# In the second round, the adding transfers of the first weights' lower parts are ordered behind the token gather on GpSimd

## The chip, the cores and the metric

The kernel runs on one core of a Trainium2 chip. The metric is the device time of one execution in microseconds (us). Five engines with a queue of instructions each work in order: TensorE (PE in the profile, its weight loads PEld), VectorE (DVE), ScalarE (ACT), GpSimd (POOL) and SyncE (SP). SyncE starts plain transfers; GpSimd starts indexed ones (gather, scatter) and those that add to what the destination holds. An engine waits for another, or for a transfer, by semaphores.

## What is computed

The reference is an attention followed by a mixture of experts:

```python
scores = scale * np.matmul(q, k.transpose(0, 1, 3, 2))
...
attn = np.exp(scores)
attn = attn / (np.sum(attn, axis=-1, keepdims=True) + 1e-09)
...
order = np.argsort(-flat)
for idx in order:
    tok, e = (int(idx) // E, int(idx) % E)
    if assigned[tok] >= 0 or counts[e] >= cap:
        continue
    assigned[tok] = e
    counts[e] += 1
...
for e in range(E):
    mask = assigned == e
    h = np.maximum(x[mask] @ w1[e], 0.0)
    out[mask] = h @ w2[e]
```

There are 4608 tokens of 512 numbers, 8 experts with 1024 hidden units, and each expert takes exactly 576 tokens. Attention masks are a window of 32 positions, or a dilated one (every fourth of 128).

## The kernel before

The attention fills the first 205 us or so and leaves its result xd in HBM. Then come eight rounds, numbered r = 0 to 7 in the code; the second round is r = 1. Each finds the next expert that fills up (`search`: counts on TensorE from flags G that VectorE makes, eight times in a row, each waiting for the other), lists its 576 tokens (`settle`, `listing`: the index list idx), fetches them (`gather`, line 1258: five indexed transfers xg, four of 128 rows and one of 64), transposes them on TensorE (line 1272, into the one buffer ptx), splits them into a high part xh (ScalarE) and the rest xl (VectorE), and runs two matrix products: the first with w1 into ph (line 1309), the second with w2 into py (lines 1351 to 1356). Results y go out by an indexed store each (line 1377). The search for round r + 1 runs while round r computes, so while TensorE still does the second product of r = 0, the tokens and first weights of r = 1 come in.

Every weight tile is split as well: raw is loaded by SyncE (line 1159), ScalarE makes the high part h (w1h, w2h), and the lower part l (w1l, w2l) is raw - h. For the three sets in `ADDED`, w2 of r = 0 and w1 and w2 of r = 1, ScalarE writes -h into l (line 1167) and GpSimd starts a transfer that adds raw to it (line 1169); the others are subtracted on VectorE. In the round r = 1 the loads of w1 from the fifth tile on (`AHEAD_W`), and all of SyncE's loads behind them, stand behind a gate: a one-element MEMSET on GpSimd (line 1150) that waits for the second gather to be issued.

The order of instructions on an engine is not written by hand. `op(engine, cost, fn, deps, boost)` notes an operation; `Schedule.run` goes through a modelled time and takes, for each engine, the ready operation with the earliest due time. A due time is the modelled end less `left`, the longest chain of costs and latencies that still follows the operation, less its boost. So an operation that gains a follower becomes due earlier. `deps` also becomes a wait where the program needs one; for an order between two instructions of one engine none is needed.

Of the buffers that the loads fill, eight raw buffers serve w1, four serve w2; a raw buffer is free again when the adding transfer has read it (`use.append(lo)`).

Of the kernel before, what the change touches and what calls it, by code (L numbers as in the profile page):

```python
# [14 lines left out]
OP = mybir.AluOpType  # L15
# [16 lines left out]
NM = 5  # L32
# [6 lines left out]
B_L, B_G, B_T, B_X, B_H, B_HL, B_Y, B_S, B_W = 23000, 27000, 15000, 0, 20000, 17000, 28000, -15000, 1500  # L39
RAW1, D_R, NQ, AHEAD_W = 8, 262, (2, 2), (3, 4)  # L40
ADDED, T_A, T_G = (("2", 0), ("1", 1), ("2", 1)), 4500, 4500
# [114 lines left out]
class Schedule:  # L156
# [8 lines left out]
    def op(self, eng, cost, fn, deps=(), boost=0, lat=0, dma=0, buf=None):  # L165
        x = Op(len(self.ops), eng, cost, fn, deps, boost, lat, dma, buf)
        for d in x.deps:
            d.users.append(x)
        self.ops.append(x)
        return x  # L170
# [940 lines left out]
def moe(tc, ctx, C, R, xd, w1, w2, out):  # L1111
    nc = tc.nc
# [7 lines left out]
    op = K.op  # L1120
# [22 lines left out]
    E, gemm1_end, x_users, got, gate = {}, {}, {}, {}, {}  # L1143

    def weights(n, r, f, deps):

        raw, old, use = RAW[n].take()
        if n == "1" and r < len(AHEAD_W) and f == AHEAD_W[r]:

            gate[r] = op("POOL", 100, lambda: nc.gpsimd.memset(raw[:1, :1], 0.0), [got[r, 1], *old], B_G)  # L1150
        if r in gate:
            deps = [*deps, gate[r]]

        def load():
            if n == "1":
                src = w1[bass.ds(E[r], 1), f].rearrange("o p d f -> p (o d f)")
            else:
                src = w2[bass.ds(E[r], 1), f * 128:f * 128 + 128, :].rearrange("o p d -> p (o d)")
            nc.sync.dma_start(raw, src)

        ld = op("SP", 60, load, [*deps, *old], dma=T_W)
        h, oldh, useh = WH[n].take()
        l, oldl, usel = WL[n].take()
        hi = op("ACT", 525, lambda: act(h, raw), [ld, *oldh], B_W)
        if (n, r) in ADDED:
            use.append(hi)
            ne = op("ACT", 525, lambda: nc.scalar.activation(l, h.bitcast(F32), AF.Copy, scale=-1.0), [hi, *oldl], B_W)
            useh.append(ne)
            lo = op("POOL", 1040, lambda: nc.gpsimd.dma_start(l, raw, accum_op=OP.add), [ne], B_W, lat=T_A)
            use.append(lo)  # L1170
        else:
            lo = op("DVE", 600, lambda: sub(nc.vector, l, raw, h), [ld, hi, *oldl], B_W)
            use += [hi, lo]
        useh.append(lo)
        return h, l, hi, lo, useh, usel
# [216 lines left out]
    def round_(r):  # L1392
        e = None
        if r:
            e = search(r) if r < NE - 1 else chain("DVE", 650, R.last, [st["fetch"], st["need"]])
        en = st["fetch"] = EN[r] = op("SP", 100, lambda: fetch(r, R.eidx), [e])
        ix, BOX[r] = settle(r, e)
        X[r] = gather(r, ix, BOX[r])
        W[r] = [weights("1", r, f, [en]) for f in range(NF)]

    round_(0)
    for r in range(NE):
        W2 = [weights("2", r, f, [EN[r]]) for f in range(NF)]
        expert(r, X[r], BOX[r], W[r], W2)
        if r + 1 < NE:
            round_(r + 1)
# [78 lines left out]
```

## Time and profile before

| | us |
|---|---|
| median of 3 runs (lowest, highest) | 705.41 (704.57, 706.64) |
| the profiled execution, its own time | 708.44 |
| its span, from the first to the last instruction | 706.6 |
| mean granted clock of TensorE | 0.972 |
| TensorE busy | 665.0 |
| VectorE busy | 484.7 |
| ScalarE busy | 291.4 |
| GpSimd busy | 140.6 |

The span is what the profile's views cover; its own time holds 1.84 us around it. Times in the rows are us from the start of the span. A granted clock of 1.00 is 2.4 GHz, 0.50 is 1.2 GHz. In the timeline a row is one instruction, or several of one kind (x9), and brackets give the idle time of the engine before it and who ended that.

### The profile page before, as it was taken

How to read it: one execution, taken by the hardware profiler on the slowest of the kernel's cores; microseconds unless marked ns; L12 is line 12 of the kernel's file. 1: busy time of each engine (PE TensorE's matmuls, PEld its weight loads, DVE VectorE, ACT ScalarE, POOL GpSimd, SP SyncE). 2: the span in 40 equal slices, each digit the busy share in tenths (PEclk: the TensorE clock that was granted, in tenths of full speed). 3: DMA queues.
4: the chain of work that ended last, by engine and by line, in shares of the span. 5: the costliest groups of instructions: out<-in, count | busy, mean ns of one | idle time of the engine just before them, and what ended most of it. 6: DMA issues, size and time to landing. Idle time of an engine off the chain costs nothing.

```text
span 706.6 us, 17388 instructions
## 1 busy us (share of the span) xinstructions
PE 665.0 (94%) x6579; PEld 585.0 (83%) x6581; DVE 484.7 (69%) x2086; ACT 291.4 (41%) x616; POOL 140.6 (20%) x206
## 2 busy tenths in 40 slices
PE   7899999999974899899999999999999999999995
PEld 5787899888963698699889889879978988988983
DVE  5467877789457889588689879969978854724200
ACT  3344554453521474286335434423524525424210
POOL 6111111100000332452410410310321131211011
PEclk9999999999985899999999999999999999999998
DMA  9999999973211684889314514512711574113001
GB/s 253 266 265 284 279 311 255 264 202 80 63 41 45 194 177 112 249 174 268 98 53 137 180 51 130 185 43 73 239 51 53 164 261 147 50 58 98 1 23 45
DMA packets 58524, 104.60 MB, mean 148 GB/s; under 512 B 6212, under 2 KB 27844, under 8 KB 58436
## 3 DMA queue, kind: packets, MB, share of 16 engines
q1 hardware_dynamic: 49096, 78.32, 38.7%
q0 software_dynamic: 9344, 25.17, 13.4%
q8 instruction: 51, 0.84, 0.5%
q14 instruction: 33, 0.27, 0.1%
HBM read 78.31 MB, written 18.87 MB: 138 GB/s over the span
## 4 chain that ended last, share of the span: by engine, by line
PE 68%; issue 12%; DVE 10%; POOL 3%; DMA 3%; ACT 1%; another core or an unknown queue 1%; POOLq 0%; SPq 0%; DVEq 0%
PE py L1351 18%; PE ph L1309 17%; PE pS L506 9%; PE px L514 6%; PE px L564 3%; PE pS L503 3%; PE pm L486 2%; PE ptx L1272 2%; PE pz L782 2%; PE py L1354 1%; PE py L1356 1%; POOL out L1377 1%; DVE hb L1329 1%; DVE G L796 1%; DMA qs<-in_qd 1%
## 5 line engine op out<-in xcount | busy, mean ns | idle before, releaser
L1351 PE MATMUL py<-w2h,hb 128*128 128x512 f32 x512 | 172.0, 401 | 0.0
L1309 PE MATMUL ph<-xh,w1h 128*128 128x256 f32 (+1 forms) x512 | 138.1, 300 | 0.0
L1309 PE MATMUL ph<-xl,w1h 128*128 128x256 f32 (+1 forms) x512 | 136.8, 298 | 0.0
L1309 PE MATMUL ph<-xh,w1l 128*128 128x256 f32 (+1 forms) x512 | 136.0, 296 | 0.0
L1351 PEld LDWEIGHTS py<-w2h,hb 128*128 128x128 f32 x512 | 96.7, 189 | 19.4
L1351 PE MATMUL py<-w2l,hb 128*128 128x512 f32 x256 | 100.2, 392 | 0.0
L1141 ACT ACTIVATE hb<-ph 128x256 fp32r<-128x256 f32 (+2 forms) x192 | 59.6, 345 | 88.5 <-PE ph L1309 86.9
L1309 PEld LDWEIGHTS ph<-xh,w1h 128*128 128x128 f32 x512 | 91.8, 190 | 0.5
L1309 PEld LDWEIGHTS ph<-xh,w1l 128*128 128x128 f32 x512 | 91.8, 190 | 0.1
L1309 PEld LDWEIGHTS ph<-xl,w1h 128*128 128x128 f32 x512 | 91.4, 190 | 0.1
L506 PE MATMUL pS<-q,k 128*80 128x96 f32 (+1 forms) x672 | 83.0, 265 | 0.0
L1377 POOL DMA_INDIRECT out<-y,idx x40 | 41.3, 1034 | 194.6 <-ACT y L1141 136.0
L456 ACT ACTIVATE E<-pS 96x384 f32<-96x384 f32 (+1 forms) x96 | 46.5, 486 | 75.2 <-PE pS L506 74.1
L1329 DVE SCALAR_TENSOR_TENSOR hb<-ph,hb 128x320 fp32r<-128x320 f32 (+1 forms) x128 | 57.0, 452 | 29.4 <-ACT hb L1141 25.2
L506 PEld LDWEIGHTS pS<-q,k 128*80 128x80 f32 (+1 forms) x672 | 68.5, 158 | 0.0
L1141 ACT ACTIVATE y<-py 128x512 f32<-128x512 f32 (+1 forms) x40 | 23.8, 596 | 104.0 <-PE py L1351 90.5
L493 DVE CUSTOM_DVE_ANT_0 junkm<-pm,const 128x80 bf16<-128x80 f32 (+1 forms) x336 | 59.5, 244 | 4.2 <-PE pm L486 3.6
L1351 PEld LDWEIGHTS py<-w2l,hb 128*128 128x128 f32 x256 | 48.6, 190 | 8.5
L514 PE MATMUL px<-v,E 81*64 81x65 f32 (+1 forms) x1344 | 47.9, 225 | 5.3 <-issue 2.9
L1258 POOL DMA_INDIRECT xg<-xd,idx x40 | 42.1, 1054 | 52.7 <-PE ph L1309 25.1
L514 PEld LDWEIGHTS px<-v,E 81*64 81x64 f32 (+1 forms) x1344 | 42.8, 138 | 10.2 <-issue 3.8
L1141 ACT ACTIVATE w1h<-raw 128x512 fp32r<-128x512 f32 x64 | 39.6, 628 | 27.6 <-DMA raw<-in_moe_w 27.2
(179 smaller groups left out, 1009.5 us busy)
## 6 DMA issues: line engine op xcount, KB each, us to landing
raw<-in_moe_w SPq DMA_DIRECT2D x128, 256.0 KB, 4.6
v<-in_vp SPq DMA_DIRECT2D x8, 780.0 KB, 14.2
v<-in_vd SPq DMA_DIRECT2D x8, 650.0 KB, 10.3
xd<-xs SPq DMA_DIRECT2D x16, 288.0 KB, 7.5
xd<-xs SPq DMA_DIRECT2D x32, 144.0 KB, 9.2
w2l<-raw POOLq DMA_DIRECT2D x16, 256.0 KB
qs<-in_qp SPq DMA_DIRECT2D x7, 576.0 KB, 10.1
k<-in_kp SPq DMA_DIRECT2D x7, 576.0 KB, 9.7
```

Of the source, the lines that this page charges most:

```text
L456: e = self.op("ACT", 380, lambda j=j, pS=pS: nc.scalar.activation(self.E[:self.nk, j * self.gs:j * self.gs + self.gs], pS.tile[:, :self.gs ...
L493: nc.vector.tensor_tensor_reduce(out=jk[:, c - c0, :nk], in0=pm[:, (c - c0) * nk:(c - c0 + 1) * nk], in1=mm[:, min(1, (c if self.kind == 0 ...
L503: nc.tensor.matmul(pS[:nk, c - c0], ls[:64 + n, c], self.r[:64 + n, :2 * nq], start=(c == c0), stop=False, skip_group_check=True)
L506: nc.tensor.matmul(pS[:nk, c - c0], self.Ks[c], self.Qm[c], start=False, stop=True, skip_group_check=True)
L514: nc.tensor.matmul(px[64 * a:64 * a + 64, c - c0], lh, self.V[c][a], start=True, stop=True)
L564: nc.tensor.transpose(t[:, c], src, C["identf"])
L1141: act = lambda o, i, f=AF.Copy: nc.scalar.activation(o, i, f)
L1258: nc.gpsimd.indirect_dma_start(out=xg[:n], out_offset=None, in_=xd, in_offset=bass.IndirectOffsetOnAxis(ap=box[0][:n, m:m + 1], axis=0))
L1309: nc.tensor.matmul(o, a[:, d * 128:d * 128 + 128], b[:, d, c0:c1], start=((d, i) == pairs[0]), stop=((d, i) == pairs[-1]))
L1329: hl = op("DVE", 335 if j == 0 else 400, lambda: nc.vector.scalar_tensor_tensor(hb[:, CAP + c0:CAP + c1], o, 0.0, hb[:, c0:c1], op0=OP.max ...
L1351: nc.tensor.matmul(py, x, w, start=(f + i == 0), stop=(f == NF - 1 and i == 2))
L1377: s = nc.gpsimd.indirect_dma_start(out=out, out_offset=bass.IndirectOffsetOnAxis(ap=box[0][:n, m:m + 1], axis=0), in_=y[:n], in_offset=None)
```

## The change

One line of `weights` gets one more dependence: the adding transfers of w1 (only r = 1 has them) now depend on the last of the round's five gathers, `got[r, NM - 1]`.

```diff
@@ -1166,7 +1166,9 @@
             use.append(hi)
             ne = op("ACT", 525, lambda: nc.scalar.activation(l, h.bitcast(F32), AF.Copy, scale=-1.0), [hi, *oldl], B_W)
             useh.append(ne)
-            lo = op("POOL", 1040, lambda: nc.gpsimd.dma_start(l, raw, accum_op=OP.add), [ne], B_W, lat=T_A)
+
+            behind = [got[r, NM - 1]] if n == "1" else []
+            lo = op("POOL", 1040, lambda: nc.gpsimd.dma_start(l, raw, accum_op=OP.add), [ne, *behind], B_W, lat=T_A)
             use.append(lo)
```

The lines behind the edit carry numbers higher by 2 in the new kernel (1169 is 1171, 1258 is 1260, 1309 is 1311). The orders of TensorE, VectorE and SyncE are the same as before, instruction by instruction. Two engines have another order, both in the round r = 1 only.

GpSimd, around the store of r = 0's second result (y_3272). w1l_3239 to w1l_3254 are lower parts (3239 the first tile of w1), xg_3255 to xg_3259 the five gathers, y the results that are stored, raw_3215 the gate. Before:

```order
L1169 DMA w1l_3239<-raw_3211 128x512
L1169 DMA w1l_3240<-raw_3212 128x512
L1169 DMA w1l_3241<-raw_3213 128x512
L1376 MEMSET spacer 1x1
L1377 DMA out<-y_3272,idx 4608x512
L1258 DMA xg_3255<-xd,idx 128x512
L1258 DMA xg_3256<-xd,idx 128x512
L1258 DMA xg_3257<-xd,idx 128x512
L1258 DMA xg_3258<-xd,idx 128x512
L1258 DMA xg_3259<-xd,idx 64x512
L1150 MEMSET raw_3215 1x1
L1169 DMA w1l_3242<-raw_3214 128x512
```

And now, from the same store on:

```order
L1379 DMA out<-y_3272,idx 4608x512
L1260 DMA xg_3255<-xd,idx 128x512
L1260 DMA xg_3259<-xd,idx 64x512
L1260 DMA xg_3256<-xd,idx 128x512
L1260 DMA xg_3257<-xd,idx 128x512
L1260 DMA xg_3258<-xd,idx 128x512
L1378 MEMSET spacer 1x1
L1379 DMA out<-y_3273,idx 4608x512
L1150 MEMSET raw_3215 1x1
L1171 DMA w1l_3239<-raw_3211 128x512
L1171 DMA w1l_3240<-raw_3212 128x512
L1171 DMA w1l_3241<-raw_3213 128x512
```

Three adds have moved from ahead of the gathers to behind the gate; the short gather, which the adds now follow, goes second instead of fifth; and the store of y_3273, which stood behind the fourth add, stands ahead of the gate.

ScalarE, where the tokens of r = 1 come in (w1h and w2h are high parts, w1l the negated ones, y results of r = 0, xh transposed tokens). Before:

```order
L1141 ACTIVATE w1h_3227<-raw_3215 128x512
L1141 ACTIVATE y_3271<-py_3209 128x512
L1167 ACTIVATE w1l_3243<-w1h_3227 128x512
L1141 ACTIVATE w1h_3228<-raw_3216 128x512
L1141 ACTIVATE xh<-ptx_3210 128x4x128
L1167 ACTIVATE w1l_3244<-w1h_3228 128x512
```

And now:

```order
L1141 ACTIVATE y_3271<-py_3209 128x512
L1141 ACTIVATE w1h_3227<-raw_3215 128x512
L1167 ACTIVATE w1l_3243<-w1h_3227 128x512
L1141 ACTIVATE xh<-ptx_3210 128x4x128
L1141 ACTIVATE w1h_3228<-raw_3216 128x512
L1167 ACTIVATE w1l_3244<-w1h_3228 128x512
```

The copy of y and the tokens' xh have each moved ahead of a weight's copy that waits for a load.

ScalarE further on, in the first product of r = 1 (hb_3264 and hb_3265 are hidden tiles of the fourth and fifth weight tile), as a piece of the difference:

```order
 L1141 ACTIVATE hb_3264<-ph_3205 128x256
-L1141 ACTIVATE w2h_3237<-raw_3221 128x512
 L1141 ACTIVATE hb_3264<-ph_3207 128x320
 L1141 ACTIVATE hb_3264<-ph_3207 128x64
-L1167 ACTIVATE w2l_3253<-w2h_3237 128x512
+L1141 ACTIVATE w2h_3237<-raw_3221 128x512
 L1141 ACTIVATE hb_3265<-ph_3204 128x256
+L1167 ACTIVATE w2l_3253<-w2h_3237 128x512
```

The copy w2h_3237, which waits for a load, has moved behind the second half of a hidden tile, and its negation behind the first half of the next one.

## Rows read from the trace of the kernel before

**Rows 1.** The page's first lines: the span, and the busy time of each engine.

```profile
span 706.6 us, 17388 instructions
...
PE 665.0 (94%) x6579; PEld 585.0 (83%) x6581; DVE 484.7 (69%) x2086; ACT 291.4 (41%) x616; POOL 140.6 (20%) x206
```

**Rows 2.** The list of waits, TensorE alone, from 240 us on: who waited for whom, us in total, how often, the longest. The first two entries.

```profile
PE pz L782 <- DVE G L796: 2.7, 1, 2.7
PE pz L1028 <- DVE ge L991: 0.6, 1, 0.6
```

**Rows 3.** The timeline of TensorE in the round r = 1 (start, us, line, output<-inputs, idle before it and who ended it).

```profile
289.11 0.46 PE L782 MATMUL pz<-G,ohr 128*128 128x64 bf16 x9
289.41 0.63 PE L1272 MATMUL ptx<-const,xg 128*128 128x128 f32 x4
...
294.78 0.46 PE L782 MATMUL pz<-G,ohr 128*128 128x64 bf16 x9 [2.66 <-DVE G L796]
295.71 1.11 PE L1272 MATMUL ptx<-const,xg 128*128 128x128 f32 x4 [0.47 <-DVE xl L1142]
...
304.92 0.64 PE L1309 MATMUL ph<-xh,w1l 128*128 128x256 f32 x4
...
323.63 0.19 PE L1028 MATMUL pz<-ge,const 128*128 128x72 bf16 x1 [0.62 <-DVE ge L991]
```

**Rows 4.** The timeline of VectorE there: the index list, the flags G, and the first step of a search round (Q).

```profile
283.16 0.33 DVE L1106 SCALAR_TENSOR_TENSOR idx<-t 64x5 int32<-64x5 f32 x2
...
288.02 0.82 DVE L796 SCALAR_TENSOR_TENSOR G<-V,delta,const 128x576 bf16<-128x576 f32 x1
...
292.63 0.32 DVE L819 STREAM_TRANSPOSE Q<-pz 128x128 f32<-128x128 f32 x1 [3.65 <-remote]
...
293.90 0.82 DVE L796 SCALAR_TENSOR_TENSOR G<-V,delta,kb 128x576 bf16<-128x576 f32 x1
```

**Rows 5.** The timeline of ScalarE there.

```profile
287.26 0.60 ACT L1141 ACTIVATE y<-py 128x512 f32<-128x512 f32 x1 [1.62 <-PE pz L782]
292.69 0.60 ACT L1141 ACTIVATE xh<-ptx 128x512 fp32r<-128x512 f32 x1 [4.83 <-remote]
...
297.35 0.63 ACT L1141 ACTIVATE w1h<-raw 128x512 fp32r<-128x512 f32 x1
299.07 0.60 ACT L1141 ACTIVATE y<-py 128x512 f32<-128x512 f32 x1 [1.09 <-PE py L1351]
...
300.09 0.62 ACT L1141 ACTIVATE w1h<-raw 128x512 fp32r<-128x512 f32 x1
...
305.14 0.62 ACT L1141 ACTIVATE w1h<-raw 128x512 fp32r<-128x512 f32 x1
...
320.14 0.63 ACT L1141 ACTIVATE w2h<-raw 128x512 fp32r<-128x512 f32 x1 [2.38 <-DMA raw<-in_moe_w]
320.68 0.53 ACT L1141 ACTIVATE hb<-ph 128x320 fp32r<-128x320 f32 x2
```

**Rows 6.** Stretches of 2 us: from:to, length, busy us (and count) of PE, PEld, DVE, ACT and POOL, granted clock, mean busy share of the 16 DMA engines, GB/s.

```profile
280.00:282.00 2.00, 2.00 (x26) 1.58 (x25) 1.93 (x6) 1.97 (x4) 1.46 (x3) 1.00 1.02 193
282.00:284.00 2.00, 2.00 (x10) 1.60 (x10) 1.68 (x11) 0.68 (x2) 1.42 (x4) 1.00 1.04 180
...
294.00:296.00 2.00, 0.75 (x11) 0.61 (x11) 1.93 (x6) 0.00 (x0) 0.00 (x0) 0.77 1.07 312
296.00:298.00 2.00, 2.00 (x8) 1.71 (x7) 1.86 (x9) 1.12 (x2) 0.00 (x0) 0.50 1.02 394
298.00:300.00 2.00, 2.00 (x15) 1.36 (x14) 0.32 (x1) 0.93 (x2) 0.00 (x0) 0.88 0.83 311
300.00:302.00 2.00, 2.00 (x19) 1.56 (x16) 1.50 (x9) 1.95 (x5) 0.99 (x3) 1.00 0.05 19
```

**Rows 7.** The timeline of GpSimd: adds (L1169), stores (L1377), gathers (L1258) and the gate (L1150).

```profile
278.61 0.88 POOL L1169 DMA_DIRECT2D w1l<-raw  x1
...
281.34 0.85 POOL L1169 DMA_DIRECT2D w1l<-raw  x1 [0.54 <-ACT w1l L1167]
...
282.50 1.04 POOL L1377 DMA_INDIRECT out<-y,idx  x1 [0.28 <-issue]
283.84 1.03 POOL L1258 DMA_INDIRECT xg<-xd,idx  x1 [0.30 <-DVE A L1053]
285.18 0.96 POOL L1258 DMA_INDIRECT xg<-xd,idx  x1 [0.30 <-issue]
...
288.96 0.91 POOL L1258 DMA_INDIRECT xg<-xd,idx  x1 [0.30 <-issue]
289.86 0.09 POOL L1150 MEMSET raw<- 1x1 f32 x1
...
291.22 1.03 POOL L1377 DMA_INDIRECT out<-y,idx  x1 [0.27 <-issue]
```

**Rows 8.** The timeline of SyncE's transfers from 276.5 to 295.6 us: eight loads in one row.

```profile
289.97 5.61 SPq L1159 DMA_DIRECT2D raw<-in_moe_w  x8
```

**Rows 9.** The list of transfers issued from 289.95 to 295.5 us: queue, count, size of each, median us from issue to landing.

```profile
raw<-in_moe_w SPq DMA_DIRECT2D x8, 256.0 KB, 5.9
```

**Rows 10.** The chain of waits between 280 and 325 us in order of time (start, us, what): two pieces.

```profile
288.98 3.63 another core or an unknown queue
...
315.00 5.70 DMA w2l<-raw
```

## The prediction

> **What bounds the kernel now.** Start with the busy times: TensorE works 665.0 of 706.6 us [rows 1], so the end moves only where TensorE waits, runs at a lower clock, or gets work later. The second view is therefore its list of waits behind the attention stage. From 240 us on, where the edited stage lies, two waits lead the list: 2.7 us for the flags G and 0.6 us for the flags ge [rows 2]. The third view, TensorE's order of time, puts both into the stage where the second round's tokens and weights come in: 2.66 us before 294.78, 0.47 us before 295.71, and 0.62 us before 323.63 [rows 3]. All that the edit can win lies there: 3.75 us of waits, and what the clock loses behind them.
>
> Who ends the long wait? The counts at 294.78 wait for G, which VectorE made from 293.90 on; its chain stood until 292.63, and the trace calls the releaser "remote" [rows 4]. What that chain needed were counts which TensorE shows as done at 289.11 + 0.46 = 289.57 [rows 3], so 3.06 us passed between the recorded end and the start. ScalarE started at 292.69 in the same manner, on transposes that were done at 289.41 + 0.63 = 290.04 [rows 3, 5]. Two engines stood for signals of TensorE that came late together; no row says why. Behind it the granted clock was 0.77, 0.50 and 0.88 over three stretches of 2 us [rows 6], that is partly at 1.2 instead of 2.4 GHz: (0.23 + 0.50 + 0.12) x 2 = 1.70 us lost. The place costs 2.66 + 0.47 + 1.70 = 4.83 us in this execution.
>
> That execution took 708.44 us (706.6 of span, 1.84 around it), and the median of the runs is 705.41: 3.03 us less, about what this stall is worth. I take it that the runs shown mostly lack it.
>
> **The gather.** Three adding transfers stand before it on GpSimd, from 278.61 to 281.34 + 0.85 = 282.19. Then come one output store (282.50 + 1.04 = 283.54) and, 0.30 later, the first gather, at 283.84 [rows 7]. Without the three, the store can go once its y is there, and the gather is then held by its index list, ready at 283.16 + 0.33 = 283.49 [rows 4]. So the gather wins between 0 and 0.35 us, and I take 0.1, since a start follows its release by some 0.3 in these rows. Does anybody wait for it? The first transposes stand behind the counts of 289.11, which wait for G of 288.02 + 0.82 = 288.84 [rows 3, 4]. The path there is the search, not the gather: **0 us**. The short fifth piece now goes second, so the second, third and fourth pieces are issued about 285.18 - 283.84 = 1.34 us later [rows 7]. The second one's transposes ran at 295.71, over 9 us behind its issue, after TensorE and VectorE work: 0 us.
>
> **The four adds behind it.** The fifth piece is issued at 288.96 + 0.91 = 289.87 [rows 7]. Behind it now stands the store of y_3273, whose y is ready at 287.26 + 0.60 = 287.86 [rows 5], so it does not wait; with its 1.03 and a gap of 0.3 [rows 7] it takes 1.3. Then comes the gate (the MEMSET of raw), then four adds of 0.9 to 1.0 each: issued from about 291.0 to 295. The longest that an add took from its issue to its landing on the chain is 5.70 [rows 10], so the first is there by 297.6 (issue ends near 291.9). TensorE reads the first lower part at 304.92 [rows 3]; should TensorE come 4.83 earlier, at 300.1. Either way it is hidden: **0 us**.
>
> **The gate and the loads.** The eight gated loads start at 289.97, right behind the gate at 289.86 [rows 7, 8]. With the store ahead of the gate they start 1.2 later (1.3 less 0.1). They also meet three more adds. Those three ran when no load was moving, with the DMA share at 1.02 and 1.04 and 193 and 180 GB/s [rows 6]: 0.79 MB at 187 GB/s is 4.2 us of all DMA engines, 1.4 for each. So a load lands from 1.2 to 5.4 us later. Who sees it? A load landed 5.9 after its issue [rows 9], the first at 295.9; its first reader on ScalarE, w1h at 297.35, now stands behind the copy of y at 299.07 + 0.60 = 299.67 [rows 5]. That leaves 3.8 us for a first load that is late by 1.2 and one or two adds, 2.6 to 4.0. The fifth load (0.7 apart over 5.61 us [rows 8]) landed near 298.7 and is read at 305.14 [rows 5]: 6.4 against at most 5.4. From 300 to 302 the DMA engines stood nearly empty, 0.05 [rows 6], which takes in some of it. Cost with the stall in place: 0. Without the stall these margins shrink by up to 4.83, and ScalarE can hold the third or fourth transposed tokens for a while: at most some 2 us. A gain is excluded here, since nothing is loaded sooner. I take **0**, nearest to the rows as they stand.
>
> **ScalarE's new order.** Eleven copies and negations change places. The one place where it shows: w2h at 320.14 waited 2.38 us for its load, and the hidden copies (hb) of 320.68 stood behind it [rows 5]. In the new order they stand ahead. VectorE's chain to ge, for which TensorE waited 0.62 at 323.63 [rows 3], passes through them, but also through the next copies, which still stand behind that load. So this wins between 0 and 0.62 if the load is as early as before, and loses up to 1.2 if the gate's delay reaches it. I take **-0.2**.
>
> **Sum.** 0 + 0 + 0 - 0.2 = -0.2 us. On the profiled execution that is 708.2; on the median 705.41 it is 705.2 us. Bounds of the terms alone: -0.35 - 0.62 = -1.0, and 2.0 + 1.2 = +3.2 us. After 335 us no engine's order differs, so nothing later adds to it.
>
> **Rivals.**
> *The stall belongs to this pile of transfers (faster).* The late signals of 292.6 came while three adds, a store and five gathers had followed each other without a pause since 278.61 [rows 7], and the list has no second wait of its size [rows 2]. If the timed runs hold the stall and the shorter pile ends it, up to 4.83 goes: 705.41 - 4.83 = 700.6; half of it is 703.0. Against it: the adds now follow the gathers instead, the pile is as long, and the 3.03 us say that the timed runs lack it. 0.19.
> *The loads come too late (slower).* The adds share the DMA engines with the gated loads; ScalarE, which works in order, stands at w1h for its load with the tokens' xh behind it, TensorE runs dry at the transposes of the third or fourth piece, and a stretch at the lower clock follows. Price: 2.0 of hold and 1.70 of clock [rows 6], 709.1. It decides if a load slips by more than the 3.8 us of margin, or by about 1 if TensorE is ahead as in the timed runs. For it: the margins above are thin without the stall. Against it: xh of the third piece now stands ahead of the second load's copy. 0.15. The Trainium skill (DMA: Bandwidth & Descriptors, Queues, rings and completion order) has each DMA engine take turns between the queues that have work for it, a packet at a time. By that rule the loads get every second turn as long as the four adds last, and this rival is the likelier; the rates of rows 6, 187 GB/s with adds and 394 with loads, fit a turn of an add that is about twice as long, but no row shows how the turns fall.
> *The change does nothing at the end.* The gather is held by its index list anyway. That is the forecast with every term at 0: 705.4.
>
> **How the numbers follow.** 0.3% of the median is 2.1 us, about what a measurement of this kernel tells from no change. A rival's chance is that of passing this mark on its side. The forecast, with the third case in it, keeps 0.66; by the bounds of its terms it spans 704.4 to 708.6, with little weight above 707.5. So: 0.19 faster, 0.66 same, 0.15 slower. The range reaches from half of the first rival's gain, a little beyond 703.0, to most of the second's loss: 702.2 to 708.2.
>
> **What would show it.** Right: the first gather within 0.4 us of its place behind the index list; the gate about 1.2 us later; the adds landed well before line 1311 reads them; the copies of hb no longer behind the load near 320; TensorE's waits in the stage within 2 us of before. Wrong: TensorE waiting at the transposes or at line 1311 with the clock at 0.50 behind it, or the 2.66 us gone and the time near 701.

## The result, and the profile after

The kernel is slower, by 0.85%. After: 711.37 us, median of 20 runs (704.14 to 717.02); before, on the same chip: 704.52, median of 20 (700.48 to 708.67). The ratio is 1.0085, its 95% interval 1.0063 to 1.0107. On a second chip, with six runs, it was 1.0139 (1.0099 to 1.0179). Ratios leave out executions over 1.5% above the fastest of their kernel, here 717.02 and 716.79, and are not the quotient of the medians given. The profiled execution took 713.43 us. The page's first lines, against [rows 1]: TensorE's work is the same (0.9 us more busy time in the same 6579 instructions), the span is 5.1 us longer.

```profile
span 711.7 us, 17384 instructions
...
PE 665.9 (94%) x6579; PEld 585.9 (82%) x6581; DVE 484.9 (68%) x2086; ACT 291.9 (41%) x616; POOL 139.9 (20%) x206
```

**What TensorE waits for.** The list of waits of TensorE from 240 us on, to be held against [rows 2]:

```profile
PE pz L1028 <- DVE ge L991: 3.1, 1, 3.1
PE ph L1311 <- DVE hb L1331: 2.6, 2, 1.6
PE ph L1311 <- ACT xh L1141: 1.2, 1, 1.2
PE ptx L1274 <- DVE xl L1142: 0.5, 2, 0.3
```

The wait of 2.7 us for G, which led the list before, is gone. In its place stand waits that were not there, for hb and xh, and the one for ge, which was small. The timeline of TensorE tells where they are, against [rows 3]:

```profile
292.85 0.33 PE L1274 MATMUL ptx<-const,xg 128*128 128x128 f32 x1 [0.32 <-DVE xl L1142]
...
305.54 0.86 PE L1311 MATMUL ph<-xh,w1h 128*128 128x320 f32 x4 [1.16 <-ACT xh L1141]
...
319.49 0.42 PE L1311 MATMUL ph<-xh,w1h 128*128 128x320 f32 x1 [1.57 <-DVE hb L1331]
322.54 0.39 PE L1311 MATMUL ph<-xh,w1h 128*128 128x256 f32 x1 [1.02 <-DVE hb L1331]
326.65 0.22 PE L1028 MATMUL pz<-ge,const 128*128 128x72 bf16 x1 [3.14 <-DVE ge L991]
```

Behind the last of them the clock falls. Stretches of 2 us, columns as in [rows 6]:

```profile
324.00:326.00 2.00, 0.00 (x0) 0.00 (x0) 1.93 (x9) 1.25 (x4) 1.31 (x2) 0.92 0.75 129
326.00:328.00 2.00, 1.35 (x8) 1.34 (x8) 1.86 (x9) 0.00 (x0) 0.39 (x1) 0.50 1.03 167
328.00:330.00 2.00, 2.00 (x9) 2.00 (x9) 1.35 (x8) 1.52 (x3) 0.00 (x0) 0.50 1.10 311
330.00:332.00 2.00, 2.00 (x9) 2.00 (x9) 0.42 (x1) 0.53 (x3) 0.79 (x1) 0.50 1.05 344
332.00:334.00 2.00, 2.00 (x15) 2.00 (x15) 1.50 (x4) 1.13 (x5) 0.00 (x0) 0.87 1.05 406
```

(0.08 + 0.50 + 0.50 + 0.50 + 0.13) x 2 = 3.42 us lost at 1.2 GHz. The stage now loses 0.5 + 1.16 + 2.59 + 3.14 = 7.4 us of waits and 3.4 of clock, 10.8 in all; before it was 3.75 and 1.70 [rows 3, 6], 5.45. The difference, 5.4, is about the 5.1 us by which the span is longer.

**Who is late.** ScalarE and VectorE near 317 us:

```profile
317.18 0.63 ACT L1141 ACTIVATE w2h<-raw 128x512 fp32r<-128x512 f32 x1 [5.63 <-DMA raw<-in_moe_w]
317.84 0.63 ACT L1167 ACTIVATE w2l<-w2h 128x512 fp32r<-128x512 f32 x1
318.38 0.53 ACT L1141 ACTIVATE hb<-ph 128x320 fp32r<-128x320 f32 x2
```

```profile
318.94 0.49 DVE L1331 SCALAR_TENSOR_TENSOR hb<-ph,hb 128x320 fp32r<-128x320 f32 x1 [6.06 <-ACT hb L1141]
```

ScalarE stands 5.63 us at w2h, the upper part of a tile of w2, whose load has not landed. The copies hb of hidden values, which TensorE had finished long before, stand behind it in ScalarE's order; VectorE stands 6.06 us for them, and TensorE finds no free buffer ph to write to. The chain of waits shows what the load waited for (start, us, what):

```profile
305.51 6.86 DMA w2l<-raw
312.49 7.94 DMA raw<-in_moe_w
320.46 0.64 ACT w2h L1141
...
321.66 0.37 ACT hb L1141
322.06 0.42 DVE hb L1331
```

The four raw buffers of w2 go round. An add has to land (6.86) before its buffer can take the next load (7.94), and only then do w2h, hb and the chain to ge follow.

**Where the transfers went.** Stretches of 6 us; the last three columns are the clock, the mean busy share of the DMA engines and GB/s. First before, then after:

```profile
280.00:286.00 6.00, 6.00 (x44) 4.65 (x42) 4.73 (x17) 3.81 (x6) 4.57 (x6) 1.00 0.97 193
286.00:292.00 6.00, 6.00 (x44) 4.76 (x44) 2.07 (x9) 0.60 (x1) 4.82 (x8) 1.00 0.73 199
...
298.00:304.00 6.00, 5.85 (x43) 4.05 (x41) 3.72 (x15) 4.82 (x9) 2.99 (x5) 0.96 0.60 174
304.00:310.00 6.00, 6.00 (x53) 5.83 (x54) 4.92 (x19) 4.70 (x11) 2.53 (x3) 1.00 0.84 146
310.00:316.00 6.00, 6.00 (x59) 5.80 (x58) 4.63 (x18) 4.90 (x14) 4.49 (x6) 1.00 1.10 233
316.00:322.00 6.00, 6.00 (x48) 6.00 (x47) 4.53 (x23) 3.50 (x10) 0.86 (x1) 1.00 1.08 236
```

```profile
280.00:286.00 6.00, 6.00 (x43) 4.72 (x42) 4.90 (x17) 3.88 (x6) 2.28 (x3) 1.00 0.15 55
286.00:292.00 6.00, 6.00 (x45) 4.73 (x43) 4.14 (x19) 1.20 (x2) 4.87 (x6) 1.00 0.56 165
...
298.00:304.00 6.00, 5.75 (x55) 4.83 (x54) 5.10 (x16) 4.40 (x8) 3.61 (x5) 1.00 1.10 261
304.00:310.00 6.00, 4.84 (x41) 4.53 (x40) 3.64 (x15) 5.70 (x14) 2.94 (x4) 1.00 1.10 269
```

From 280 to 292 the DMA engines had 6 x (0.97 + 0.73) = 10.2 us of work before and 6 x (0.15 + 0.56) = 4.3 after: 5.9 us have moved behind 292. The room up to a share of 1, 6 x (0.40 + 0.16) = 3.4 us from 298 to 310, is filled, and more (1.10 in both stretches); from 310 to 322 the kernel before had none (1.10 and 1.08). The list of transfers, issued from 292.05 to 296 us, and then the loads issued from 300 to 318, first before, then after:

```profile
raw<-in_moe_w SPq DMA_DIRECT2D x5, 256.0 KB, 6.6
w1l<-raw POOLq DMA_DIRECT2D x4, 256.0 KB, 9.1
```

```profile
raw<-in_moe_w SPq DMA_DIRECT2D x4, 256.0 KB, 3.8
```

```profile
raw<-in_moe_w SPq DMA_DIRECT2D x5, 256.0 KB, 7.9
```

The median add takes 9.1 us to land, and the median load of that later stretch 7.9 instead of 3.8. In two more profiles of this GpSimd order it was 6.6 (`after_again`) and 8.0 (`pool_new2`).

### The profile page after: what moved, and what is told of

Its sections match the earlier page's. It is cut to its first block, busy times and chain, and to the rows that moved or that the text cites. A ratio compares the mean times of both kernels' runs of the same rounds, so it can differ in the third digit from the quotient of the medians.

```text
span 711.7 us, 17384 instructions
## 1 busy us (share of the span) xinstructions
PE 665.9 (94%) x6579; PEld 585.9 (82%) x6581; DVE 484.9 (68%) x2086; ACT 291.9 (41%) x616; POOL 139.9 (20%) x206
## 4 chain that ended last, share of the span: by engine, by line
PE 65%; issue 13%; DVE 11%; DMA 5%; POOL 5%; ACT 1%; POOLq 0%; SPq 0%; DVEq 0%; ACTq 0%
PE ph L1311 17%; PE py L1353 16%; PE pS L506 9%; PE px L514 6%; PE px L564 3%; PE pS L503 3%; DMA raw<-in_moe_w 2%; PE pm L486 2%; PE ptx L1274 2%; POOL out L1379 2%; PE pz L782 1%; DVE hb L1331 1%; PE py L1356 1%; PE py L1358 1%; DMA qs<-in_qd 1%
## 6 DMA issues: line engine op xcount, KB each, us to landing
qs<-in_qp SPq DMA_DIRECT2D x7, 576.0 KB, 10.2
```

## The experiments

In each, the issue order of the engines is that of before or of after, row by row, but for the rows named. Rows with + and - are in an engine's issue order. All ratios are to the kernel before, on the same chip.

### Which part of the change costs the time

`adds_only`: the order of before, with only the adds moved. `act_new`: GpSimd's order of before, ScalarE's of after. `pool_rest`: GpSimd's other moves without the adds. `pool_new`: GpSimd's order of after, ScalarE's of before.

```diff
 GpSimd, round 1 (adds_only)
-DMA w1l_3239<-raw_3211 128x512
-DMA w1l_3240<-raw_3212 128x512
-DMA w1l_3241<-raw_3213 128x512
 five gathers
 MEMSET raw_3215 1x1
+DMA w1l_3239<-raw_3211 128x512
+DMA w1l_3240<-raw_3212 128x512
+DMA w1l_3241<-raw_3213 128x512
 DMA w1l_3242<-raw_3214 128x512
 GpSimd, round 1 (pool_rest)
 first gather
+fifth gather
 second to fourth gather
-fifth gather
+store of the third y
 MEMSET raw_3215 1x1
 DMA w1l_3242<-raw_3214 128x512
-store of the third y
```

> The kernel before with one thing moved: the three adds of w1 stand behind the gate instead of ahead of the gathers; gathers, store, gate and ScalarE's order stay as before. Theory DMA (the three adds, moved from a time in which the DMA engines carried nothing else into the time of the gated loads, hold up loads and later adds): ratio to before 1.006 to 1.010, the DMA share under 0.4 from 280 to 286 us and over 1.0 from 294 to 314, the longest wait of ScalarE for a load of w2 above 4 us. Theory ORDER (ScalarE's new order is what costs): ratio 0.998 to 1.002. Theory GATE (the later gate and the short gather in second place are what costs): ratio 0.998 to 1.002.

> ScalarE's order of the changed kernel, GpSimd's order of the kernel before. Theory DMA: ratio to before 0.996 to 1.001 (the hidden copies that now stand ahead of a load's copy may win a little). Theory ORDER: ratio 1.006 to 1.010. Theory GATE: ratio 0.998 to 1.002.

> The kernel before with the rest of GpSimd's change and without the adds' move: the three adds stay ahead of the gathers, the short gather goes second, the store of the third result goes ahead of the gate. Theory DMA: ratio to before 0.999 to 1.003 (loads start some 1.3 us later, nothing more). Theory ORDER: ratio 0.998 to 1.002. Theory GATE: ratio 1.006 to 1.010.

> GpSimd's whole order of the changed kernel, ScalarE's order of the kernel before. Theory DMA: ratio to before 1.007 to 1.012, no better than the changed kernel. Theory ORDER: ratio 0.998 to 1.002. Theory GATE: ratio 1.007 to 1.010.

Measured: `adds_only` 1.0084 (1.0044 to 1.0123), `act_new` 1.0023 (0.9993 to 1.0053), `pool_rest` 1.0007 (0.9974 to 1.0040), `pool_new` 1.0023 (0.9987 to 1.0059). The three adds alone lose about as much as the whole change did (1.0085); the other moves make no loss that shows. DMA holds, ORDER and GATE fall. In `adds_only` the same place fails: w2h waits 7.87 us for its load, and TensorE 3.46 for hb:

```profile
318.49 0.63 ACT L1162 ACTIVATE w2h<-raw 128x512 fp32r<-128x512 f32 x1 [7.87 <-DMA raw<-in_moe_w]
```

```profile
319.90 0.58 PE L1335 MATMUL ph<-xh,w1h 128*128 128x256 f32 x1 [3.46 <-DVE hb L1355]
```

`pool_new` came out below what DMA asked for, though its profile held the same waits. So it was run again, beside the kernel after itself:

> The kernel after once more, beside the others of this call on the same chip. If the loss measured first is that of the order and not of that chip: ratio 1.005 to 1.011, and the profile again has PE waiting 2 us or more in sum for hb, xh and ge from 304 to 328 us. Rival (the loss comes and goes with the chip): ratio below 1.004.

> The kernel with GpSimd's order of after and ScalarE's order of before once more, whose first interval (0.999 to 1.006) left open whether ScalarE's new order takes part. Theory TRAFFIC (GpSimd's order makes the loss by itself): ratio 1.005 to 1.010, as after on the same chip. Rival BOTH (about half of the loss is ScalarE's): 1.000 to 1.004 with after at 1.006 or more.

`after_again` 1.0139 (1.0099 to 1.0179), more than was expected, and `pool_new2` 1.0101 (1.0053 to 1.0148). The profile of `after_again` again has TensorE waiting, 2.8 us for hb, 2.5 for ge and 0.6 for xh, with w2h 6.33 us behind its load. The loss isn't one chip's, and GpSimd's order makes it by itself. Whether ScalarE's new order adds a little, these intervals don't tell.

### Traffic, or the lateness of what was moved

`after_thin` and `before_thin`: the three adds move 16 columns of 512. `after_other`: three other adds of the crowded stretch are cut instead. In these three a part of the lower parts' computation is left out. `adds_two`: before, two of the three adds moved. `before_load`: the order of before kept, and three adds more, of 2.25 adds' bytes in all, into a tile that nothing reads.

```diff
 after_thin, before_thin (tiles 0 to 2 of w1); after_other (tiles 4, 5 of w1, 0 of w2)
-nc.gpsimd.dma_start(l, raw, accum_op=OP.add)
+nc.gpsimd.dma_start(l[:, :16], raw[:, :16], accum_op=OP.add)
 GpSimd, round 1 (before_load)
 MEMSET raw_3215 1x1
 DMA w1l_3242<-raw_3214 128x512
+DMA spare<-const 128x384 x3
```

> Edit: the kernel after, but the adding transfers of the first three lower parts of w1 in round 1 move 16 columns of 512 and not all; the lower parts are then mostly left at minus the upper part, so this run leaves part of the computation out. Every instruction keeps its place. Theory TRAFFIC (what the change costs is the transfer time of these adds, laid on the loads of 292 to 318 us): PE's waits of 305 and 319 to 327 us and the clock drop there go; latencies of the adds and loads issued from 292 to 302 us fall from 9 to 10 us to 6 or less; 702 to 705 us, ratio to before 0.991 to 0.999. Theory ORDER (the late gathers and the gate behind them, or ScalarE's new order, cost the time): as after, 709 to 713 us, ratio 1.005 to 1.011, with w2h still waiting over 4 us for its load near 317 us.

> Edit: the kernel before, with the same three adding transfers cut to 16 columns (the same part of the computation left out). Theory PILE (the 2.66 us wait of PE at 292.6 us is made by the traffic of these adds ahead of the gathers): the wait falls below 0.6 us and no clock drop follows it; 702 to 705 us, ratio 0.991 to 0.999, about as the thinned kernel after. Theory CHANCE (the wait comes of something else in this stretch, as the number of transfers that GpSimd has issued, not their bytes): a wait of 1 to 2.7 us at the same place stays, 705 to 709 us, ratio 0.997 to 1.003.

> Edit: the kernel before, with only the second and third of the three adds moved behind the gate; the first stays ahead of the gather. Theory TRAFFIC with PILE (bytes ahead of the gather make the wait at 293 us, bytes behind make those of 305 to 327 us, each in proportion): a wait at 293 us of 0.5 to 1.5 us, waits and clock loss of 305 to 327 us at about two thirds of those of all three moved (3.9 us with clock), 707 to 711 us, ratio 1.001 to 1.006. Rival THRESHOLD (any two adds more are already too many behind the gate): as all three moved, 710 to 713 us, ratio 1.006 to 1.011.

> Edit: the kernel before, its whole order kept, with three adding transfers more (128 x 384 each, into a tile that nothing reads) right behind the first add that follows the gate, near 290 us, and one memset of that tile at the start of the stage: the traffic of 2.25 adds without moving anything that the products need. Theory TRAFFIC (the change loses by the transfer time that it lays on 292 to 318 us): loads and adds there take 8 us or more to landing, PE waits for hb, xh or ge 2 us or more in sum from 300 to 330 us, ratio 1.004 to 1.010. Rival LATE PARTS (it loses because the moved lower parts themselves, or what is ordered behind them, come late): nothing that is read is later, ratio 0.998 to 1.003.

> Edit: the kernel after, with three other adds cut to 16 columns of 512: w1's tiles 4 and 5 and w2's tile 0 of round 1, which it issues from 297.95 to 302 us; the three moved ones are whole (part of the computation is left out). Theory TRAFFIC (what counts is how much is moved from 292 to 318 us, not which transfers): as when the moved ones are cut, ratio 0.997 to 1.003, no wait of PE over 1 us from 300 to 330 us. Rival FIRST FOUR (the four adds side by side at 292 us hold the gate's loads, whatever follows): ratio 1.006 to 1.012.

Measured: `after_thin` 1.0001 (0.9978 to 1.0024), `after_other` 1.0012 (0.9984 to 1.0040), `before_load` 1.0048 (1.0019 to 1.0077), `adds_two` 1.0006 (0.9978 to 1.0035), `before_thin` 0.9996 (0.9967 to 1.0024).

Cutting the moved adds takes the loss away, and so does cutting three others that were not moved; adding traffic without moving anything makes a loss. With the adds cut, the loads issued from 300 to 318 us landed in 3.4 us (`after_thin`) and 3.1 (`after_other`), against 7.9. So it is the amount moved from 292 to 318 us, not the lateness of the moved parts, and not the four adds side by side. FIRST FOUR and LATE PARTS fall. Two details came out otherwise than expected. `after_other` has a wait of 1.5 us for xh near 305 us, where none over 1 was expected; a wait like it stands in the kernel after (1.16) and, below, in a kernel that loses nothing (1.1), so by itself it does not make the loss. `before_load` lost less in its profile than expected: the loads issued from 300 to 318 us took 4.9 us and not 8 or more, w2h waited 2.72 us, TensorE 1.05 for ge.

```profile
313.90 0.63 ACT L1169 ACTIVATE w2h<-raw 128x512 fp32r<-128x512 f32 x1 [2.72 <-DMA raw<-in_moe_w]
```

`adds_two` speaks against a loss in proportion: two adds cost nothing that can be measured, three cost 6 us, and two thirds of 1.0084 would be 1.0056, outside its interval. THRESHOLD falls; of the proportional expectation, 1.001 to 1.006, the part up to 1.0035 is left, so this rests on two ratios from different chips and is not firm.

`before_thin` tells of the wait for G of [rows 3]. With next to no bytes in front of the gather it stays:

```profile
294.97 0.64 PE L803 MATMUL pz<-G,ohr 128*128 128x64 bf16 x9 [2.73 <-DVE G L817]
```

PILE, as a matter of bytes, falls. Neither thinned kernel beats the kernel before; my 0.991 to 0.999 for them was wrong.

### What passes the late loads on to TensorE

`after_hb`: the kernel after, with the upper and negated parts of w2's last four tiles behind the next hb copies. `before_load_hb`: the same edit on `before_load`.

```diff
 ScalarE, round 1 (the first two of four places)
-ACTIVATE w2h_3235<-raw_3219 128x512
-ACTIVATE w2l_3251<-w2h_3235 128x512
 ACTIVATE hb_3263<-ph_3206 128x320
 ACTIVATE hb_3263<-ph_3206 128x64
-ACTIVATE w2h_3236<-raw_3220 128x512
-ACTIVATE w2l_3252<-w2h_3236 128x512
 ACTIVATE hb_3264<-ph_3205 128x256
+ACTIVATE w2h_3235<-raw_3219 128x512
+ACTIVATE w2l_3251<-w2h_3235 128x512
 ACTIVATE hb_3264<-ph_3207 128x320
 ACTIVATE hb_3264<-ph_3207 128x64
 ACTIVATE hb_3265<-ph_3204 128x256
+ACTIVATE w2h_3236<-raw_3220 128x512
+ACTIVATE w2l_3252<-w2h_3236 128x512
```

> Edit: the kernel after, with ScalarE's upper and negated parts of the last four w2 tiles of round 1 put behind the hb copies of the next one or two hidden tiles. Theory QUEUE (the late load costs TensorE time only because hb copies that are ready stand behind the waiting w2h in ScalarE's order): the waits for hb of 1.57 and 1.02 us, the 3.14 us for ge and the clock drop at 325.7 us go or shrink below 1 us in sum, while the load stays as late; the wait of 1.16 us at 305 us stays; 704 to 708 us, ratio 0.997 to 1.003. Rival LATER (w2's late loads then hold the second matrix product): PE waits 2 us or more for w2l or w2h between 325 and 345 us, 708 to 713 us, ratio 1.003 to 1.011.

> Edit: as the run with the three transfers more, and ScalarE's upper and negated parts of the last four w2 tiles of round 1 behind the next hb copies. Theory QUEUE (late loads cost time by the copies that stand behind them on ScalarE): at least half of the loss of the run without this goes, ratio 0.998 to 1.004. Rival LOADS (the late loads are waited for directly): as the run without, within 0.002 of its ratio.

> The kernel after with ScalarE's reordering of the w2 tiles once more, beside the others on this chip; its first profile had a wait of 1.69 us for G which took TensorE off the crowded stretch. Theory QUEUE: also in a profile without that wait no hb wait over 1 us from 305 to 330 us; ratio 0.998 to 1.004, clearly below the 1.0085 and 1.014 of the kernel after. Rival RELIEF (the wait for G had made room, not the reordering): ratio 1.006 or more.

Measured: `after_hb` 1.0002 (0.9978 to 1.0025), again as `after_hb2` on another chip 1.0008 (0.9983 to 1.0034); `before_load_hb` 1.0004 (0.9974 to 1.0033) against 1.0048 without. The adds stay behind the gather, and the loss is gone. The first profile had a wait of 1.69 us for G ahead of the stretch; the second had none, and still no hb wait. Its list of waits from 240 to 345 us, ScalarE's row that was 5.63 late, and two stretches of 6 us:

```profile
PE ph L1335 <- ACT xh L1162: 1.1, 1, 1.1
PE ptx L1298 <- DVE xl L1163: 0.5, 1, 0.5
PE ptx L1298 <- issue: 0.2, 1, 0.2
```

```profile
314.52 0.63 ACT L1162 ACTIVATE w2h<-raw 128x512 fp32r<-128x512 f32 x1 [1.52 <-DMA raw<-in_moe_w]
```

```profile
298.00:304.00 6.00, 4.94 (x45) 4.57 (x46) 4.11 (x14) 4.56 (x10) 2.62 (x4) 1.00 1.09 289
304.00:310.00 6.00, 6.00 (x51) 5.90 (x50) 4.68 (x21) 5.08 (x12) 4.17 (x7) 1.00 1.12 224
```

The DMA engines are as full as after the change, 1.09 and 1.12, and ScalarE still waits for a load, but what TensorE needs no longer stands behind it. The loads issued from 300 to 318 us took 6.0 us there, near the 6.6 of `after_again`. QUEUE holds; LATER, LOADS and RELIEF fall. The same edit on the kernel before was not run; in that kernel's profile TensorE waited only 0.62 us behind these copies, for ge, so there is little that it could win there.

### The wait for G

Of [rows 3] was left open why VectorE starts on pz 3.06 us after its recorded end. `turn_late`: the kernel before, with the transposes that stand directly behind that pz two hidden tiles later on TensorE. `hb_turn`: the same on `after_hb`.

```diff
 TensorE, round 1, third search step
 MATMUL pz<-G,ohr 128x4x16
-MATMUL ptx_3210<-const_63,xg_3255 128x128 x4
 products py of two hidden tiles
+MATMUL ptx_3210<-const_63,xg_3255 128x128 x4
 products py of the next hidden tile
```

> Edit: the kernel before, with TensorE's transposes of the first token tile of round 1 put behind the next two hidden tiles' products and no longer directly behind the third search step's matmul (pz). Theory HELD (the signal of pz reaches VectorE 2 to 3 us after its modelled end because the transposes stand directly behind it): VectorE's Q follows pz within 0.3 us, the wait for G near 294 us falls below 0.6 us, no clock drop follows; 702 to 705 us, ratio 0.992 to 0.998. Rival ELSEWHERE (the late signal has another cause): a wait of 1 to 2.7 us for G stays in the profile, ratio 0.997 to 1.003.

> Edit: the kernel after with both reorderings: the last four w2 tiles' upper and negated parts behind the next hb copies on ScalarE, and the transposes of the first token tile two hidden tiles later on TensorE. If HELD is right: no wait for G near 294 us and none over 1 us from 305 to 330 us, 702 to 705 us, ratio 0.992 to 0.998, faster than both kernels. If ELSEWHERE: as with ScalarE's reordering alone, ratio 0.998 to 1.003.

`turn_late` 1.0017 (0.9986 to 1.0048); `hb_turn` 1.0055 (1.0028 to 1.0081), slower, as neither theory expected, with a new wait of 1.7 us for xl, which now comes later. In `turn_late` the wait for G was 1.02 us, and VectorE still started late:

```profile
285.21 0.46 PE L803 MATMUL pz<-G,ohr 128*128 128x64 bf16 x9
...
289.29 0.45 PE L803 MATMUL pz<-G,ohr 128*128 128x64 bf16 x9 [1.02 <-DVE G L817]
```

```profile
287.14 0.32 DVE L840 STREAM_TRANSPOSE Q<-pz 128x128 f32<-128x128 f32 x1 [2.19 <-PE pz L803]
```

287.14 is 1.47 behind 285.21 + 0.46. HELD falls; the cause stays open. What the profiles do show first: the kernel after and `after_hb` have the same order on every engine up to 311 us, and VectorE's start on this pz, recorded as done at 289.68 and 292.82, came at 289.72 in the one and at 294.91 in the other:

```profile
289.22 0.46 PE L782 MATMUL pz<-G,ohr 128*128 128x64 bf16 x9
...
289.72 0.32 DVE L819 STREAM_TRANSPOSE Q<-pz 128x128 f32<-128x128 f32 x1 [0.87 <-PE pz L782]
```

```profile
292.36 0.46 PE L803 MATMUL pz<-G,ohr 128*128 128x64 bf16 x9
...
294.91 0.32 DVE L840 STREAM_TRANSPOSE Q<-pz 128x128 f32<-128x128 f32 x1 [2.92 <-remote]
```

So one order gives either, from one execution to the next.

Second, the profiles of all eighteen kernels and repeats, one for each, set side by side. In the eight that keep at least one of the three adds ahead of the gathers, VectorE started on this pz 1.42 to 3.13 us after its recorded end, and TensorE waited 1.0 to 2.7 us for G. Of the ten with all three behind the gate, eight show 0.04 to 0.59 us and no such wait over 0.5; `after_thin` and `after_hb` show 2.05 and 2.09, with waits of 1.6 and 1.7. So the wait goes with the place of the adds, though not strictly, and not with their bytes: it stays in both thinned kernels. What joins the two is not known. Nor does a gain from it show at the end: the profile of `after_hb2` has neither this wait nor those for hb and ge, and its runs are level with the kernel before.

No version beat the kernel before; those with the hb copies ahead came level with it, but for `hb_turn`.

## Why the prediction was wrong

705.2 us and no change were said, with 702.2 to 708.2 as the range; the time is 711.37. Step by step:

- **The gather.** Said: up to 0.35 us earlier. It came 0.60 later, at 284.44 against 283.84 [rows 7], though the store ahead of it was done by 282.90; 1.54 us of "issue" lie between, and no row tells why. Nobody waits for it, as said, so the term of 0 holds.

```profile
281.87 1.03 POOL L1379 DMA_INDIRECT out<-y,idx  x1 [3.05 <-DVE Lt L1020]
284.44 1.05 POOL L1260 DMA_INDIRECT xg<-xd,idx  x1 [1.54 <-issue]
...
292.09 0.09 POOL L1150 MEMSET raw<- 1x1 f32 x1
292.12 3.68 POOL L1171 DMA_DIRECT2D w1l<-raw  x4
```

- **The four adds behind it.** The step took 5.70 us from issue to landing, from an add of [rows 10] that had less company. Measured: 9.1, the median of the four. The readers of these adds did not wait, which the step had said, but it looked at no other reader.
- **The gate and the loads.** This step failed: it put the cost of the moved transfers at 0. It had the gate 1.2 us later, and it was 2.2 (292.09 against 289.86 [rows 7]). That was not the loss: the first load landed 3.84 after its issue at 292.21, near 296.05, hardly later than the 295.9 of the step. The step followed the eight gated loads to their first readers, found margins of 3.8 and 6.4 us and stopped there. The transfers behind them, the adds of w2 and the loads that wait for their buffers, it did not follow, and these were late, at 317 us. It also let the nearly empty stretch of 300 to 302 [rows 6] take in some of the moved work; the 6 us stretches show 3.4 us of room from 298 to 310 for 5.9 us that came.
- **ScalarE's new order.** Said: -0.2, at most 1.2 lost. The step had the mechanism, an hb copy behind a w2h that waits for its load [rows 5], and priced it by the gate's delay alone, 1.2, though the step on the loads had let a load be up to 5.4 late. With loads of 7.9 us the wait at w2h rose from 2.38 to 5.63, and the waits of TensorE for hb and ge from 0.62 to 5.7, with 3.4 of clock behind. The experiments on hb show that this copy's place is what passes the loss on.
- **"The runs shown mostly lack it"**, the stall of 4.83. This can't be settled from the runs: the 3.03 us that it rests on are less than the 4.83, the eight profiles of orders with adds ahead all have the wait, and none of the runs without a profile can be asked.

Of the rivals, *the loads come too late* was right in kind: crowded transfers, ScalarE held in order, the clock falling. Its place was wrong (w2's tiles and hb near 317 us, not w1h and the transposed tokens) and its price of 3.7 us too low: the medians differ by 6.9. Of the prediction's signs of being wrong, TensorE waiting at line 1311 with the clock at 0.50 behind it came true. The rule of the Trainium skill (DMA: Bandwidth & Descriptors, Queues, rings and completion order) by which queues take turns pointed to this rival. The trace agrees in the sum: with the moved adds in the stretch, loads took 6.6 and 7.9 us against 5.9 [rows 9] and 3.8; no row shows the turns. *The stall belongs to this pile* was right in that the profile after lacks the stall, and most profiles with the adds behind lack it too; but it isn't the adds' bytes (`before_thin`), and no run shows a gain from it.

## What to carry to other kernels

When transfers are moved in time, compare what the DMA engines must do in the stretch they move into with the room left there (5.9 us against 3.4 here), over the whole stretch and not over its emptiest 2 us, and follow every ring of buffers that refills there to its last reader. On an engine that works in order, put copies that are ready ahead of those that wait for a load: that took the loss of a crowded stretch away without taking a byte out of it. A delay that leads the list of waits in one profile may be gone in the next execution of the same order (VectorE 2.09 us late in one and 0.04 in another here); a gain is not to be counted on it.

## What was not expected of the hardware

- Adding transfers of 256 KB needed 9.1 us to land (median of four) where loads ran beside them, against 5.70 [rows 10].
- The loss did not look in proportion to the bytes: two adds moved gave 1.0006 on one chip, three 1.0084 on another.
- A result of TensorE was taken up by VectorE 0.04 us after its recorded end in one execution and 2.09 us after it in another, with the same order of all engines up to there; in the kernel before it was 3.06. Neither fewer bytes nor another neighbour on TensorE did away with it.
